# Fewer units with 16-row inverses in a chunked linear recurrence, and new step lists around it

## The chip, the core and the metric

The kernel runs on one core of one Trainium2 chip. The metric is the device time of one execution in microseconds (us). PE is TensorE (matmuls; PEld its weight loads), DVE VectorE, ACT ScalarE, POOL GpSimd, SP the queue that issues the DMAs. The granted clock is TensorE's clock as a share of its full 2.4 GHz.

## The reference

Three stages follow each other. The first is the one that the change touches; per batch b (4), head h (8) and step t of 768, with a state of 40 x 40:

```
y[t]  = r[t] @ state
Sa    = state @ a[t]
state = state * w[t] - outer(Sa, b[t]) + outer(v[t], k[t])
```

The second mixes positions and channels: u = x + (xT U V)T, then u + relu(u W1) W2, with U and V of rank 32 and 4 x 320 hidden channels. The third is an attention with four experts, of which each position takes two. U, V, W1 and W2 arrive as 64-bit floats and are converted on the chip.

## The kernel before

**Units and chunks.** The sequence is cut into 12 chunks of C = 64 steps. A chunk has two units, one per pair of batches: unit u belongs to chunk c = u // 2, and there are NU = 24. A unit holds 16 heads (8 columns p of 2 partition halves r). Four units make a group g (GU = 4), so chunks 0 and 1 are group 0, chunks 2 and 3 group 1, and so on to group 5.

**front(u)**, line 153 on, needs no state. Its 9 pieces are: the decay product Q by a scan (line 164), the inverse decay G (172), ga (177), bkt (180), all on DVE; then transposes of G (188) and of bkt (198) on PE; then the two 32 x 32 diagonal blocks and the block below them, pd (215), copied by ACT into LX, m21 and, for groups below HALVES, los (217 to 220); then pk (227), which POOL masks (230). Loads for unit u + 2 are issued along the way.

**lanes(g)**, line 233, inverts the triangular blocks of a whole group on DVE. After a transpose (237) each step s multiplies and adds (249, 251), one block per partition lane, and it ends with memsets and a transpose into tf (262). With g < HALVES a 32 x 32 block is treated as two 16 x 16 blocks, m = 2, and there are 14 steps; otherwise 30. Every yield ends a step.

**core(u)**, line 265, is the part that carries the state. pw (275) takes the old state X and v. Then, for the first and the second 32 rows (i = 0, 1): with g < HALVES a product with the 16-row inverse (pa, 297), a copy into U (300), a product with the block los between the halves (304), a copy into w (307), and in either form the product with tf (311) and a copy into U (314). For i = 1 the product with m21 (287) stands first. At the end px (321, 326) adds up the new state and DVE scales it into sv (328), which the next chunk's pw reads. That makes 10 steps with HALVES covering g, and 6 without.

**outs(u)**, line 332, has 6 steps and makes the output: transposes pv (339), pz (347), pn (360) masked by DVE into uvt (363), py (372, 376) scaled into x (380).

**The order** is written out by hand. PE, DVE, ACT and POOL run their instructions in program order; only the DMA issues on SP are placed by the framework. For each chunk a string gives the steps: A and B are the cores of the two units, p and q the outs of the two batch pairs (behind by one chunk and more), f the next piece of the fronts of later units, u the next weight conversion, x the products with U. Behind each letter that the second string names, one step of the oldest unfinished lanes is taken. A group's lanes become available with the last front piece of its fourth unit (line 405); what of it is left when its first chunk begins is run in one go (line 447). FIRST holds chunks 0 to 3, STEADY 4 to 6, TAIL 7 to 11. The front of the first four units and lanes(0) run before the first chunk.

**Weight conversions**, Mix.weights (line 545): 15 of them before the recurrence ends. Step u number i issues the load of the next one, finishes the one before (511, then its put: an ACT copy and a POOL subtraction), and converts its own: four DVE instructions (500, 501, 504, 505), an ACT one (502) and a POOL addition (506), which the next step's 511 waits for. The last one is finished after the recurrence.

Of the kernel before, what the change touches and what calls it, by code (L numbers as in the profile page):

```python
# [15 lines left out]
AF = mybir.ActivationFunctionType  # L16
# [12 lines left out]
PP = 8  # L29
WLEN = PP * (C + 1)  # L30
LDW = 3 * PP * C + WLEN
HP = PP // 2
GU = 4
# [5 lines left out]

HALVES = 2
FIRST = (('ABffABffABfffABffABffABfffABffABfffABABffff', ''),
         ('ABppffABfABppffABfABqqfABffABqqfABfppABABfffff', 'Ap'),
         ('ABqqfABppfABffABppfABfABqqfABffABqqppfABABfffff', 'AB'),
         ('ABqqfABppABfABppfABfABqqABfABqqppfABABffff', 'AB'))
STEADY = ('ABqqppfABfppfABfqqABfqqppfABABffff', 'ABf')
TAIL = (('ABqqppfABfppfABfqqABfqqppfABABffffu', 'ABf'),
        ('ABuqqppABuppABuqqABqqppABAB', 'ABp'), ('ABuqqppABuppABuqqABqqppABAB', 'ABp'),
        ('ABuqqppuxABuppxxABuqquxABqqppxABABxx', 'ABp'), ('ABuqqppuxABuppxABuqqxABqqppABAB', 'ABp'))  # L50


def recurrence(ctx, tc, ld, vin, rv, ident, xs, keep, wpool, mix):

    nc = tc.nc
# [53 lines left out]
    def zeros():  # L109

        for t in [x[:, 0] for x in sv[:2]] + [x[:, :, :, D:] for x in uv] + sbd + rpt:
# [3 lines left out]
    xf = [x.rearrange("p c f -> p (c f)") for x in xs]  # L115
    o = NC // 4 * DM
    los = [x[:, a:a + PP * 32].rearrange("p (q t) -> p q t", t=32)
           for a in [o + LDW + PP * 32 * k for k in range(3)] + [o + LDW - PP * 32] for x in xf]

    def edges(ts):  # L120
        for t in ts:
            nc.gpsimd.memset(t[:, :, :16], 0.0)

    edges(los[:6])

    BK, GA, PC, LX, M21, TF = {}, {}, {}, {}, {}, {}

# [15 lines left out]
    def copy_v(u):  # L143
        for r in range(2):
            z = slice(64 - 64 * r, 128 - 64 * r)
            nc.scalar.activation(uv[u % 4][z, :, r, :D], sv[u % 4][64 * r:64 * r + 64, 1], AF.Copy)
# [6 lines left out]
    def front(u):  # L153
# [64 lines left out]
        nc.scalar.activation(m21, pd[:, :, 1], AF.Copy)  # L218
        if g < HALVES:
            nc.scalar.activation(los[u][:, :, 16:], pd[:, :, 0, 16:], AF.Copy)  # L220
# [12 lines left out]
    def lanes(g):  # L233
# [3 lines left out]
        nc.vector.transpose(Lf, LX[g].rearrange("p t x -> p (t x)"))  # L237
        m = 2 if g < HALVES else 1
        h = 32 // m
# [25 lines left out]
    def core(u):  # L265

        g, uu = divmod(u, GU)
        c, bp = divmod(u, NBP)
        ga, bk, tf, X, U = GA[u], BK[u], TF[g], sv[u % 4], uv[u % 4]
        pw = ps.tile([128, PP, D], F32, tag=f"c{bp}", bufs=1, name=f"pw{u}")  # L270
        for p in range(PP):
            for k in range(2):
                for r in range(2):
                    q = slice(64 * r, 64 * r + 64)
                    nc.tensor.matmul(pw[q, p], ga[q, k, p], X[q, k, p], start=p == k == 0, stop=k == 1,  # L275
                                     skip_group_check=True)
        w0 = const.tile([128, PP, D], F32, tag="w0", bufs=2, name=f"w0{u}")
        nc.scalar.activation(w0, pw, AF.Copy)
        yield

        for i in range(2):
            qs = [slice(64 * r + 32 * i, 64 * r + 32 * i + 32) for r in range(2)]
            if i:
                for p in range(PP):
                    for r in range(2):
                        q0 = slice(64 * r, 64 * r + 32)
                        nc.tensor.matmul(pw[qs[r], p], M21[u][q0, p], U[q0, p, r, :D], start=False, stop=True,
                                         skip_group_check=True)
                nc.scalar.activation(w0, pw, AF.Copy)
                copy_v(u)  # L290
                yield
            if g < HALVES:

                pa = ps.tile([128, PP, D], F32, tag="f", bufs=6, name=f"pa{u}_{i}")
                for p in range(PP):
                    for q in qs:
                        nc.tensor.matmul(pa[q, p], tf[q.start:q.start + 16, uu * PP + p], w0[q.start:q.start + 16, p],
                                         start=p == 0, stop=True, skip_group_check=True)
                for r in range(2):
                    nc.scalar.activation(U[qs[r], :, r, :D], pa[qs[r]], AF.Copy)  # L300
                yield
                for p in range(PP):
                    for r, q in enumerate(qs):
                        nc.tensor.matmul(pw[q, p], los[u][q.start:q.start + 16, p], U[q.start:q.start + 16, p, r, :D],
                                         start=False, stop=True, skip_group_check=True)
                for q in qs:
                    nc.scalar.activation(w0[q], pw[q], AF.Copy)
                yield
            for p in range(PP):
                for r in range(2):  # L310
                    nc.tensor.matmul(pw[qs[r], p], tf[qs[r], uu * PP + p], w0[qs[r], p], start=p == 0,  # L311
                                     stop=True, skip_group_check=True)
            for r in range(2):
                nc.scalar.activation(U[qs[r], :, r, :D], pw[qs[r]], AF.Copy)
            yield
        if c < NC - 1:

            px = ps.tile([128, PP, D], F32, tag=f"c{bp}", bufs=1, name=f"px{u}")
            for r in range(2):
                q = slice(64 * r, 64 * r + 64)  # L320
                nc.tensor.matmul(px[q], ident[q, q], X[q, 0], start=True, stop=False, skip_group_check=True)
        yield
        if c < NC - 1:
            for p in range(PP):
                for r in range(2):
                    nc.tensor.matmul(px[64 * r:64 * r + D, p], bk[:, p, r], U[:, p, r, :D], start=False, stop=True,
                                     skip_group_check=True)
            nc.vector.tensor_tensor(sv[(u + NBP) % 4][:, 0], px,  # L328
                                    PC[u + NBP][:, :, None].to_broadcast([128, PP, D]), op=OP.mult)
        yield  # L330
# [52 lines left out]
    def run(*seqs):  # L383
        for seq in seqs:
            for _ in seq:
                pass
# [10 lines left out]
    def body(v):  # L397

        if v >= NU:
            return  # L400
        pieces = head(v + 1) if v != GU - 1 else iter(())
        for k in range(5):
            next(pieces, None)
            next(FR[v])
            if k == 4 and v % GU == GU - 1:
                LN.append(lanes(v // GU))
            yield

    def cores(bp):
        for u in range(bp, NU, NBP):  # L410
            yield from core(u)
# [23 lines left out]
    run(head(0))  # L435
    for v in range(GU):
        run(body(v))
    edges(los[6:])
    run(LN.pop())
    seqs = {"A": cores(0), "B": cores(1), "p": outputs(0), "q": outputs(1),  # L440
            "f": chain(head(GU), *[body(v) for v in range(GU, NU)]),
# [3 lines left out]
    for c in range(NC):  # L445
        while 2 * c // GU not in TF:
            run(LN.pop(0))
        steps, along = FIRST[c] if c < len(FIRST) else STEADY if 2 * c + AHEAD + NBP < NU else TAIL[c - NC]
        for x in steps:
# [474 lines left out]
def tile_kernel(ctx, tc, ld, vin, rin, U, V, w1, w2, qk, vg, wo, out):  # L924
# [6 lines left out]
    with ExitStack() as kctx:  # L931
# [3 lines left out]
        with ExitStack() as rctx:  # L935
            recurrence(rctx, tc, ld, vin, rin, ident, xs, keep, wpool, mix)
# [59 lines left out]
```

## Time and profile before

| what | value |
|---|---|
| three runs | 926.45, 921.86, 915.11 us; median 921.86 |
| the profiled execution | 912.26 us; its span 910.5 us |
| PE busy | 862.1 us, 95% of the span |
| DVE busy | 584.5 us, 64% |
| ACT busy | 478.7 us, 53% |
| POOL busy | 217.2 us, 24% |
| mean granted clock | 0.972 |
| recurrence (to its last product) | 0 to 430.8 us |

Spans are counted from the first instruction. A row of the windows view gives a stretch, its length, the busy time of each engine with the number of instructions, the granted clock, the mean busy share of the DMA engines and their GB/s. A row of a timeline gives start, duration, engine, line, operation, output <- inputs, shapes and the count of merged instructions; in square brackets how long the engine was idle before and what ended that.

### The profile page before, as it was taken

Reading aid. Unit: us, or ns where it says so; the run is one execution under the profiler, and the core shown is the slowest. Engines: PE = TensorE matmul, PEld = TensorE weight load, DVE = VectorE, ACT = ScalarE, POOL = GpSimd, SP = SyncE. Lnnn points to the kernel's source line nnn. Section 1 sums busy time; section 2 is a strip of 40 time slices with the busy share of each in tenths; the row PEclk is TensorE's granted clock in tenths of the full one; section 3 lists DMA queues with packets and bytes.
Section 4 is the critical chain, followed back from the end, with each engine's and each line's share of the span. In section 5 each row is a group of like instructions: output and inputs, shape, how many; then the busy total and the mean of one; then the engine's idle time right before and its main releaser. Section 6 shows DMA issues by size and latency. Waiting matters only on the chain.

```text
span 910.5 us, 31479 instructions
## 1 busy us (share of the span) xinstructions
PE 862.1 (95%) x13668; PEld 736.6 (81%) x13668; DVE 584.5 (64%) x1352; ACT 478.7 (53%) x1109; POOL 217.2 (24%) x245
## 2 busy tenths in 40 slices
PE   5599999999999989999999999999999999999997
PEld 4589888899899978888777888878778889797875
DVE  8867657789879688664662423232237886878874
ACT  5386656845665535554332423222237767766772
POOL 6111111001010103441341322020122633344330
PEclk9889879999999987999999999999999999999999
DMA  5232212212221123221100010000000000010001
GB/s 164 64 109 87 62 54 62 77 54 62 84 76 38 48 66 88 81 78 55 52 29 1 22 35 1 0 1 1 1 0 2 1 30 15 2 44 1 30 15 44
DMA packets 25386, 39.51 MB, mean 43 GB/s; under 512 B 5792, under 2 KB 12576, under 8 KB 25248
## 3 DMA queue, kind: packets, MB, share of 16 engines
q1 hardware_dynamic: 25248, 37.51, 13.7%
q8 instruction: 107, 1.75, 0.8%
q14 instruction: 31, 0.25, 0.1%
HBM read 33.56 MB, written 3.93 MB: 41 GB/s over the span
## 4 chain that ended last, share of the span: by engine, by line
PE 74%; DVE 9%; ACT 7%; issue 4%; POOL 2%; DMA 1%; SPq 0%; ACTq 0%; POOLq 0%; DVEq 0%
PE pn L360 5%; PE po L891 4%; PE pw L275 4%; PE tp L878 3%; PE ph L691 3%; PE pa L710 3%; PE pa L709 3%; PE ph L688 3%; PE pa L708 3%; PE ph L689 3%; PE ph L687 3%; PE pw L311 2%; PE pb L198 2%; PE py L372 2%; PE pd L215 2%
## 5 line engine op out<-in xcount | busy, mean ns | idle before, releaser
L695 DVE SCALAR_TENSOR_TENSOR hl<-ph,hh 128x512 fp32r<-128x512 f32 x60 | 41.1, 690 | 117.1 <-ACT hh L694 116.3
L861 POOL TENSOR_TENSOR P<-P,sm 128x128 f32<-128x128 f32 (+2 forms) x92 | 82.7, 929 | 126.5 <-DVE sm L851 114.3
L230 POOL TENSOR_TENSOR ga<-ga,mask 128x512 f32<-128x512 f32 x24 | 34.1, 1422 | 263.5 <-ACT ga L229 263.5
L694 ACT ACTIVATE hh<-ph 128x512 fp32r<-128x512 f32 x60 | 35.3, 597 | 112.1 <-PE pa L710 107.0
L842 ACT ACTIVATE P<-ps,mx 128x640 f32<-128x640 f32 (+4 forms) x96 | 60.5, 634 | 22.6 <-DVE mx L840 14.6
L840 DVE CUSTOM_DVE_ANT_0 ps<-ps,neg 128x640 f32<-128x640 f32 (+4 forms) x96 | 59.1, 639 | 7.6 <-PE ps L838 6.4
L249 DVE TENSOR_TENSOR tmp<-lt 128x84 f32<-128x84 f32 (+14 forms) x148 | 55.2, 373 | 3.1
L360 PE MATMUL pn<-rpt,uvt 128*128 128x128 f32 x384 | 52.6, 294 | 4.2 <-ACT uvt L340 3.2
L878 PE MATMUL tp<-ident,P 128*128 128x128 f32 x336 | 52.0, 275 | 2.3 <-DVE sm L849 0.9
L275 PE MATMUL pw<-sv,ga 64*64 64x40 f32 x1536 | 50.3, 232 | 4.0 <-DVE sv L328 3.8
L275 PEld LDWEIGHTS pw<-sv,ga 64*64 64x64 f32 x1536 | 49.1, 142 | 5.0 <-DVE sv L328 4.4
L251 DVE TENSOR_TENSOR lt<-lt,tmp 128x84 f32<-128x84 f32 (+14 forms) x148 | 49.6, 335 | 5.1
L360 PEld LDWEIGHTS pn<-rpt,uvt 128*128 128x128 f32 x384 | 47.9, 203 | 5.7 <-ACT uvt L340 4.8
L363 DVE TENSOR_TENSOR uvt<-pn,mask 128x512 f32<-128x512 f32 x48 | 32.2, 685 | 29.6 <-PE pn L360 27.7
L878 PEld LDWEIGHTS tp<-ident,P 128*128 128x128 f32 x336 | 39.5, 140 | 9.6 <-issue 2.2
L710 PE MATMUL pa<-hh,w 128*128 128x512 f32 x120 | 47.0, 392 | 0.0
L688 PE MATMUL ph<-ul,w 128*128 128x512 f32 x120 | 46.8, 390 | 0.2 <-DVE ul L677 0.2
L709 PE MATMUL pa<-hl,w 128*128 128x512 f32 x120 | 47.0, 391 | 0.0
L687 PE MATMUL ph<-uh,w 128*128 128x512 f32 x120 | 45.8, 391 | 1.2 <-ACT uh L676 1.2
L689 PE MATMUL ph<-uh,w 128*128 128x512 f32 x120 | 46.7, 389 | 0.0
L891 PE MATMUL po<-pt,vals 128*64 128x256 f32 (+3 forms) x320 | 45.1, 397 | 0.4 <-DVE pt L884 0.4
L724 POOL TENSOR_TENSOR t<-t,ul 128x512 f32<-128x512 f32 x12 | 15.4, 1302 | 120.2 <-DVE t L723 120.1
(218 smaller groups left out, 2311.6 us busy)
## 6 DMA issues: line engine op xcount, KB each, us to landing
ld<-in_ld SPq DMA_DIRECT2D x132, 80.0 KB
sv<-in_vin SPq DMA_DIRECT2D x48, 80.0 KB
rpt<-in_rin SPq DMA_DIRECT2D x48, 80.0 KB
out<-o SPq DMA_DIRECT2D x24, 160.0 KB
ld<-in_ld SPq DMA_DIRECT2D x44, 81.2 KB
ld<-in_w SPq DMA_DIRECT2D x4, 512.0 KB
ld<-in_w SPq DMA_DIRECT2D x5, 320.0 KB
room<-in_w SPq DMA_DIRECT2D x5, 320.0 KB
```

The lines of the kernel that those rows point to most:

```text
L275: nc.tensor.matmul(pw[q, p], ga[q, k, p], X[q, k, p], start=p == k == 0, stop=k == 1, skip_group_check=True)
L360: nc.tensor.matmul(pn[:, p], ut[:, h * HP + p], rp[:, :, h * HP + p], start=p == 0, stop=True, skip_group_check=True)
L687: nc.tensor.matmul(ph, w[:, 0, f], uh[:, ft], start=ft == 0, stop=False)
L688: nc.tensor.matmul(ph, w[:, 0, f], ul[:, ft], start=False, stop=False)
L689: nc.tensor.matmul(ph, w[:, 1, f], uh[:, ft], start=False, stop=False)
L709: nc.tensor.matmul(pa[ft], w[:, o:o + m], hl, start=False, stop=False)
L710: nc.tensor.matmul(pa[ft], w[:, 2 * DM - FT[2][0] + o:2 * DM - FT[2][0] + o + m], hh, start=False, stop=last)
L840: nc.vector.tensor_tensor_reduce(ps[:, :k], ps[:, :k], neg[:, S - k:], -1.0, 3e38, op0=OP.add, op1=OP.min, accum_out=mx[:, i:i + 1])
L842: nc.scalar.activation(P[blk][:, off[i] - off[i0]:off[i + 1] - off[i0]], ps[:, :k], AF.Exp, bias=mx[:, i:i + 1], scale=-1.0, accum_out=sm[ ...
L861: nc.gpsimd.tensor_tensor(p, p, sm[:, i:i + 1].to_broadcast([128, w]), op=OP.mult)
L878: nc.tensor.transpose(pt[:, j - j0], P[:, c:c + 128], ident)
L891: nc.tensor.matmul(po[64 * r:64 * r + 64, s0:w], VS[b][:, j, HD * e:HD * e + HD], PT[r][:, j, s0:], start=j == 0, stop=j == i1 - 1, skip_g ...
```

## The change

HALVES falls from 2 to 1, so group 1 (units 4 to 7) uses 32-row inverses like the groups behind it; only group 0 keeps the 16-row form. The los tiles shrink from eight to four, and the late memset of two of them goes. In the 16-row form the two copies of pw into w, one per 32 rows, become one over all rows. The strings of chunks 0 to 3 are new: the cores of chunks 2 and 3 have 6 steps, the letters f stand at other places (24, 13, 15, 13 of them in place of 23, 16, 15, 10), and the lanes go along with more letters. In the strings of chunks 7 to 11 the letters u number 0, 2, 2, 6, 6 in place of 1, 3, 3, 5, 4.

```diff
@@ -39,15 +39,15 @@
 
 
 
-HALVES = 2
-FIRST = (('ABffABffABfffABffABffABfffABffABfffABABffff', ''),
-         ('ABppffABfABppffABfABqqfABffABqqfABfppABABfffff', 'Ap'),
-         ('ABqqfABppfABffABppfABfABqqfABffABqqppfABABfffff', 'AB'),
-         ('ABqqfABppABfABppfABfABqqABfABqqppfABABffff', 'AB'))
+HALVES = 1
+FIRST = (('ABfffABfffABfffABfffABfffABfffABfffABfffABAB', 'AB'),
+         ('ABppffABfABppffABfABqqfABfABqqfABfppABABfff', 'ABpq'),
+         ('ABqqppffABfppffABfqqfABfqqppffABABfffff', 'ABf'),
+         ('ABqqppffABfppfABfqqfABfqqppfABABfffff', 'ABf'))
 STEADY = ('ABqqppfABfppfABfqqABfqqppfABABffff', 'ABf')
-TAIL = (('ABqqppfABfppfABfqqABfqqppfABABffffu', 'ABf'),
-        ('ABuqqppABuppABuqqABqqppABAB', 'ABp'), ('ABuqqppABuppABuqqABqqppABAB', 'ABp'),
-        ('ABuqqppuxABuppxxABuqquxABqqppxABABxx', 'ABp'), ('ABuqqppuxABuppxABuqqxABqqppABAB', 'ABp'))
+TAIL = (('ABqqppfABfppfABfqqABfqqppfABABffff', 'ABf'),
+        ('ABuqqppABppABuqqABqqppABAB', 'ABp'), ('ABuqqppABppABuqqABqqppABAB', 'ABp'),
+        ('ABuqqppuxABuppxxABuqquxABuqqppxABABxx', 'ABp'), ('ABuqqppuxABuppuxABuqqxABuqqppABAB', 'ABp'))
 
 
 def recurrence(ctx, tc, ld, vin, rv, ident, xs, keep, wpool, mix):
@@ -115,13 +115,13 @@
     xf = [x.rearrange("p c f -> p (c f)") for x in xs]
     o = NC // 4 * DM
     los = [x[:, a:a + PP * 32].rearrange("p (q t) -> p q t", t=32)
-           for a in [o + LDW + PP * 32 * k for k in range(3)] + [o + LDW - PP * 32] for x in xf]
+           for a in [o + LDW + PP * 32 * k for k in range(HALVES * GU // 2)] for x in xf]
 
     def edges(ts):
         for t in ts:
             nc.gpsimd.memset(t[:, :, :16], 0.0)
 
-    edges(los[:6])
+    edges(los)
 
     BK, GA, PC, LX, M21, TF = {}, {}, {}, {}, {}, {}
 
@@ -303,8 +303,7 @@
                     for r, q in enumerate(qs):
                         nc.tensor.matmul(pw[q, p], los[u][q.start:q.start + 16, p], U[q.start:q.start + 16, p, r, :D],
                                          start=False, stop=True, skip_group_check=True)
-                for q in qs:
-                    nc.scalar.activation(w0[q], pw[q], AF.Copy)
+                nc.scalar.activation(w0, pw, AF.Copy)
                 yield
             for p in range(PP):
                 for r in range(2):
@@ -435,7 +434,6 @@
     run(head(0))
     for v in range(GU):
         run(body(v))
-    edges(los[6:])
     run(LN.pop())
     seqs = {"A": cores(0), "B": cores(1), "p": outputs(0), "q": outputs(1),
             "f": chain(head(GU), *[body(v) for v in range(GU, NU)]),
```

## Rows read from the trace of the kernel before

**Rows 1.** windows, chunks 0 to 4 and 8 to 11: us, then busy by engine.
```profile
41.90:72.44 30.54, 29.76 (x920) 26.44 (x920) 20.41 (x25) 25.12 (x63) 3.82 (x3) 0.86 0.35 101
72.44:111.87 39.43, 38.13 (x1091) 34.54 (x1086) 26.93 (x50) 26.47 (x63) 4.01 (x3) 0.91 0.25 72
111.87:155.78 43.91, 42.14 (x1186) 37.87 (x1184) 29.80 (x59) 27.11 (x63) 4.80 (x3) 0.88 0.20 59
155.78:192.35 36.57, 35.09 (x1110) 31.45 (x1108) 28.22 (x62) 24.65 (x58) 2.53 (x2) 1.00 0.21 63
192.35:221.37 29.02, 28.99 (x857) 26.38 (x854) 26.32 (x56) 17.07 (x41) 2.60 (x2) 1.00 0.24 71
...
307.65:333.70 26.05, 21.72 (x633) 19.80 (x629) 23.38 (x61) 12.51 (x28) 4.28 (x6) 1.00 0.27 79
333.70:365.69 31.99, 31.01 (x633) 28.73 (x633) 25.89 (x56) 13.98 (x30) 7.30 (x6) 0.68 0.25 66
365.69:392.40 26.71, 26.05 (x663) 21.35 (x661) 18.75 (x35) 15.48 (x34) 11.30 (x13) 1.00 0.31 92
392.40:430.82 38.42, 36.23 (x886) 31.98 (x884) 18.80 (x33) 18.50 (x40) 10.13 (x12) 1.00 0.19 61
```

**Rows 2.** windows, the stretches after a TensorE stall.
```profile
118.40:129.00 10.60, 10.54 (x228) 9.56 (x230) 4.63 (x6) 6.11 (x15) 0.00 (x0) 0.52 0.22 65
333.70:354.00 20.30, 20.30 (x336) 19.42 (x338) 14.72 (x33) 6.61 (x14) 4.51 (x4) 0.51 0.24 63
```

**Rows 3.** timelines of VectorE and then TensorE, end of chunk 8.
```profile
316.39 0.35 DVE L511 SCALAR_TENSOR_TENSOR ld<-Q,ld 128x192 f32<-128x192 f32 x1
...
323.12 0.35 DVE L511 SCALAR_TENSOR_TENSOR ld<-invhot,ld 128x192 f32<-128x192 f32 x1
...
333.16 0.48 DVE L328 TENSOR_TENSOR sv<-px,pc 128x320 f32<-128x320 f32 x1
...
328.49 1.43 PE L326 MATMUL px<-uv,bk 128*40 128x40 f32 x64
333.70 6.91 PE L275 MATMUL pw<-sv,ga 64*64 64x40 f32 x128 [3.79 <-DVE sv L328]
```

**Rows 4.** timelines of VectorE and then TensorE, end of chunk 10.
```profile
385.25 0.49 DVE L511 SCALAR_TENSOR_TENSOR ld<-invhot,ld 128x320 f32<-128x320 f32 x1 [1.71 <-POOL ld L506]
...
390.80 1.10 DVE L328 TENSOR_TENSOR sv<-px,pc 128x320 f32<-128x320 f32 x2 [0.81 <-PE px L326]
...
392.40 3.93 PE L275 MATMUL pw<-sv,ga 64*64 64x40 f32 x128
```

**Rows 5.** timeline of TensorE in chunk 3 (start us, us, what, idle before).
```profile
152.32 0.66 PE L188 MATMUL pt<-ident,G 128*128 128x128 f32 x4
...
155.78 3.88 PE L275 MATMUL pw<-sv,ga 64*64 64x40 f32 x128
...
162.17 1.34 PE L297 MATMUL pa<-w,tf 16*32 16x40 f32 x64
...
176.94 1.66 PE L304 MATMUL pw<-uv,x 16*32 16x40 f32 x62 [0.20 <-ACT uv L300]
```

**Rows 6.** timeline of all engines, end of chunk 1 and start of chunk 2.
```profile
109.20 1.23 DVE L164 TENSOR_TENSOR_SCAN Q<-ld,onehot 128x520 f32<-128x520 f32 x1
...
112.82 2.22 POOL L230 TENSOR_TENSOR ga<-ga,mask 128x512 f32<-128x512 f32 x1 [5.63 <-ACT ga L229]
113.83 1.25 DVE L249 TENSOR_TENSOR tmp<-lt 128x28 f32<-128x28 f32 x1
...
115.12 0.19 DVE L251 TENSOR_TENSOR lt<-lt,tmp 128x28 f32<-128x28 f32 x1
...
118.46 0.76 PE L297 MATMUL pa<-w,tf 16*32 16x40 f32 x27 [1.06 <-DVE tf L262]
```

**Rows 7.** windows of chunk 4, line 249 and then line 251 alone.
```profile
192.35:221.37 29.02, 6.04 (x18) 1.00 0.24 71
...
192.35:221.37 29.02, 5.92 (x18) 1.00 0.24 71
```

## The prediction

> **What bounds the kernel now.** I read the page first (busy shares and granted clock over the span), then TensorE's waits, then a table of windows cut at the first pw matmul (line 275) of every chunk, then timelines around the waits. The windows' columns are the stretch, its length, the busy time of PE, PEld, DVE, ACT and POOL with counts, the granted clock and the DMA share and rate. The reader is to see three regions in [rows 1]. In a steady chunk (4) TensorE is busy for 28.99 of 29.02 us and VectorE for 26.32, so TensorE bounds it with VectorE close behind. Chunks 0 to 3 take 30.54 + 39.43 + 43.91 + 36.57 = 150.45 us; here units 0 to 7 use the 16-row form and the clock is below full in three of them. Chunks 8 to 11 hold no front, yet take 26.05 + 31.99 + 26.71 + 38.42 = 123.17 us, and chunk 9 at clock 0.68 does the same TensorE work as chunk 8.
>
> A low clock is dear. After two stalls the granted clock stands near 0.5, the 1.2 GHz level, for most of 10.6 and 20.3 us [rows 2]. The pw group takes 6.91 us there [rows 3] and 3.93 us at full clock [rows 4], 1.76 times, so each microsecond at the low level loses 0.43. From the mean clocks the time at the low level was 2(1 - 0.91) x 39.43 = 7.1 us in chunk 1, 10.5 in chunk 2 and 20.5 in chunk 9, and the losses are 3.1, 4.5 and 8.8 us.
>
> **Part 1: units 4 to 7 lose the 16-row steps.** Each chunk 2 and 3 drops two pa groups (1.34 us for 64 matmuls) and two los groups (1.34 to 1.9 us; one is in the rows) [rows 5]: about 5.8 us of TensorE per chunk, 11.6 in all, on the engine that bounds. Their copies go too: 16 ScalarE copies per chunk of some 0.43 us, which TensorE sometimes waited for (0.20 us at the los group [rows 5]). Chunk 2 also loses its first stall, 1.06 us for the transposed inverses tf [rows 6], because the new lists finish group 1's inverse inside chunk 1; with that stall goes the low clock behind it, 4.5 us.
>
> The price is VectorE. A 32-row inverse has 30 steps of two instructions where the 16-row one has 14. In chunk 4, 18 such steps took 6.04 + 5.92 us [rows 7], 0.66 a step, 0.72 with the gap between instructions. All of group 1's steps but four now fall in chunk 1: 26 x 0.72 = 18.7, with the closing transpose and memsets 21.3 us, in place of 9.0 now (13 small steps and the opening transpose). One front costs VectorE 4.63 us, from 109.20 to 113.83 [rows 6], and TensorE 3.46, from 152.32 to 155.78 [rows 5]; a step "f" is a fifth: 0.92 and 0.70.
>
> **Part 2: the lists of chunks 0 to 3.** Steps "f" per chunk go from 23, 16, 15, 10 to 24, 13, 15, 13.
> Chunk 0: one more f (+0.7), and no f is left behind the last A and B, so the new state sv, which now queues on VectorE behind group 1's opening transpose and two steps, is bare: +1.2. Bounds: 0 if VectorE is early, +3.8 if sv is as late as in chunk 8 [rows 3]. I take +1.9.
> Chunk 1: VectorE needs 26.93 - 9.0 - 3 x 0.92 + 21.3 = 36.4 us. TensorE at full clock needs 38.13 - 3.1 - 2.1 = 33. VectorE takes over. At the share that it reaches in chunk 4 (0.91) that is 40; with its waits for ScalarE and TensorE I take 42, +2.6. Bounds 36.4 and 49.
> Chunk 2: 43.91 - 1.06 - 4.5 - 5.8 = 32.5 for TensorE; VectorE has some 28, but bunched in the second half with group 2's steps: +1.5. I take 34, -9.9.
> Chunk 3: 36.57 - 5.8 - 1.1 (ScalarE waits) + 2.1 = 31.8 for TensorE; VectorE 28.22 + 2.8 = 31, at 0.91 34. I take 34, -2.6.
> The sum is -8.0. The single w copy in group 0 in place of two saves 0.43 us of ScalarE four times a chunk in chunks 0 and 1, beside other work; two memsets fewer on GpSimd at the start are 0.2 us each, off the path. Both at nothing: TensorE or VectorE covers them, and without the cover they would give back 3.4 and 0.4 us. The loads that the fronts issue on SP move with them by at most three f; they stay two units ahead.
>
> The row at the end of chunk 1 shows a step of 28 elements taking 1.25 us while GpSimd's masking ran, and its partner 0.19 without [rows 6]. The Trainium skill (SBUF — State Buffer, Who interferes with whom) says that a VectorE instruction with two SBUF inputs and a GpSimd instruction reading SBUF exclude each other; the trace agrees. By that rule each of chunk 1's three maskings could now hold one step for another 1.06 us, and the chunk would be 45 and not 42.
>
> **Part 3: conversions of the last chunks.** The 16 steps u go from 1, 3, 3, 5, 4 (chunks 7 to 11) to 0, 2, 2, 6, 6.
> Chunk 8: the last sv starts on VectorE some 3 us after px ended, and TensorE stands for 3.79 us [rows 3]. Of VectorE's work ahead of it two conversions go, 316.39 to 318.66 and 323.12 to 325.98, 5.1 us, and the first one (1.3) comes in. VectorE then still waits for TensorE's pn at 318.4, so sv moves by 2.7 us, not 3.8, and 1.1 us of stall stays: -2.7.
> Chunk 9: if the clock holds, -8.8.
> Chunk 10: six conversions instead of five, and larger ones, 15.7 us against 12.1. VectorE was already waiting 1.71 us for GpSimd inside one, and had only 0.81 us to spare before sv [rows 4]. The extra one stands ahead of the uvt masking and sv: 2.2 us of its own, 1.2 of wait for GpSimd, 1.2 from the larger ones, less 0.8, is 3.8; part is gained where VectorE now idles. I take +3, bounds 0 and +5.
> Chunk 11: two more conversions, 5.5 us, ahead of the last py products, where VectorE idles up to 4 us at a time: +3, bounds 0 and +5.5.
> A stall of 3 us before chunk 11 may drop the clock: 0 to 8.8, at even odds for the lesser loss seen (4.5): +2.5. The sum is -3.0.
>
> **Total.** -8.0 - 3.0 = -11 us. The profiled execution took 912.26 us (span 910.5 and 1.8 around it) and would take 901; the median of the three runs shown is 921.86, 9.6 us more. Against the median: 911 us.
>
> **Rivals.**
> A, both regions come out clean: chunks 0 to 3 reach their floors, 31.3 + 36.4 + 32.5 + 31.8 = 132, -18.5; the tail gives -3.8 - 8.8 + 3 = -9.5. That is -28 and 894 us. For it: chunk 4 runs with no stall at 0.91 of VectorE. Against: chunk 1 would want VectorE without a gap. Chance 0.22.
> B, the stall is only moved: chunk 10 now ends as chunk 8 did and chunk 11 runs at the low clock for the whole 20.5 us: +6.3 on the forecast, 917 us. For it: the 0.81 us of slack. Against: stalls of about 1 us in chunks 9 and 11 left the clock full. Chance 0.17.
> C, slower: in chunk 1 TensorE waits for VectorE so often that the clock goes to the low level and stays. Its 33 us then become 33 x 1.76 = 58, +16 on my 42, and the total is +5: 927 us. It decides from 26 us at the low level on (11/0.43). For it: shorter stalls brought 7 to 10 us in chunks 1 and 2. Against: a slow TensorE is a busy one, and after 10 us the clock came back. Chance 0.10.
> The forecast, 911, keeps 0.51, with its own range 903 to 918.
>
> **How the numbers follow.** The measurement tells about 2% from no change, 18.4 us here, so faster means under 903.4. A gives most of its chance, the forecast a little: 0.25. Slower by 2% means over 940.3, beyond C: 0.04, for a C with a poor tail. Within 2%: 0.71. The range 896 to 926 leaves out half of A and half of C.
>
> **What would show it.** Right: no line 297 in chunks 2 and 3; 30 steps of line 249 in chunk 1 or just before it, VectorE over 0.85 busy there; no stall for tf at chunk 2's start; full clock in chunk 9; a longer TensorE wait for sv at the end of chunk 10. Wrong: chunk 1 under 38 us (towards A) or over 48 at a low clock (C), chunk 9 still at a low clock, or chunk 11 over 45 us (B).

## The result, and the profile after

The changed kernel took 913.26 us (median, 901.82 to 917.2) and the kernel before 920.97 (915.11 to 926.45), 14 runs each on one chip: 7.7 us less between the medians. The ratio is 0.9892, interval 0.9858 to 0.9925: 9.9 us less (6.9 to 13.1), faster by 1% and within the 2% that count as no change. The ratio leaves out the five longest runs of the changed kernel (915.44 to 917.2 us) as slow ones and none of the kernel before, which widens the difference. The forecast was 911, with a range of 896 to 926.

The profiled execution took 914.89 us, its span 913.2 us. Its page gives the busy times from TensorE to GpSimd:

```profile
PE 858.9 (94%) x13156; PEld 731.5 (80%) x13156; DVE 600.6 (66%) x1383; ACT 460.6 (50%) x1065; POOL 215.8 (24%) x241
```

TensorE is busy for 3.2 us less than before and VectorE for 16 us more. From line 307 on the code's line numbers are one lower than before, from 438 on two lower (sv is L327, pn L359, the finishing step of a conversion L509).

The windows view, cut at the first pw of each chunk, answers to [rows 1]: chunks 0 to 4, then 8 to 11.

```profile
44.11:79.45 35.34, 32.80 (x953) 28.48 (x953) 26.85 (x32) 23.81 (x59) 5.09 (x4) 0.80 0.37 106
79.45:118.39 38.94, 36.54 (x956) 32.97 (x957) 34.60 (x81) 22.25 (x52) 2.76 (x2) 0.87 0.18 54
118.39:153.27 34.88, 31.82 (x924) 28.65 (x924) 27.41 (x48) 20.01 (x47) 3.89 (x3) 1.00 0.22 66
153.27:192.24 38.97, 37.92 (x949) 34.55 (x948) 31.37 (x68) 19.75 (x47) 2.81 (x3) 0.82 0.23 66
192.24:221.54 29.30, 29.30 (x850) 26.38 (x849) 28.13 (x59) 16.54 (x40) 2.47 (x2) 1.00 0.25 71
...
308.73:331.73 23.00, 21.89 (x639) 19.99 (x635) 19.49 (x49) 11.69 (x26) 2.31 (x3) 1.00 0.18 50
331.73:353.91 22.18, 21.82 (x632) 19.94 (x632) 18.58 (x53) 11.55 (x26) 1.95 (x3) 1.00 0.27 75
353.91:385.48 31.57, 26.60 (x663) 21.33 (x661) 23.18 (x39) 16.78 (x36) 14.08 (x13) 1.00 0.31 84
385.48:434.25 48.77, 44.76 (x884) 39.60 (x885) 25.01 (x44) 20.50 (x44) 14.65 (x18) 0.79 0.24 72
```

Chunk 2 is 9.0 us shorter and at full clock; chunk 9 is 9.8 shorter at 1.00 in place of 0.68. Chunk 10 is 4.9 longer, and chunk 11 10.3 longer at 0.79. Chunk 3 has fewer matmuls than in [rows 1], but takes longer at 0.82. A steady chunk (4) takes 29.30 us.

TensorE's waits, from its timeline (the bracket gives the idle time before and what ended it):

```profile
79.45 3.93 PE L275 MATMUL pw<-sv,ga 64*64 64x40 f32 x128 [0.82 <-DVE sv L327]
...
118.39 3.93 PE L275 MATMUL pw<-sv,ga 64*64 64x40 f32 x128 [0.68 <-DVE sv L327]
...
152.28 1.06 PE L198 MATMUL pb<-ident,bkt 128*128 128x128 f32 x8 [3.06 <-DVE bkt L180]
...
331.73 3.93 PE L275 MATMUL pw<-sv,ga 64*64 64x40 f32 x128 [0.93 <-DVE sv L327]
...
385.48 6.66 PE L275 MATMUL pw<-sv,ga 64*64 64x40 f32 x128 [2.25 <-DVE sv L327]
```

The stall for tf at the start of chunk 2 [rows 6] is gone; 0.68 us for sv is left. The 3.79 us before chunk 9 [rows 3] are 0.93. New are 3.06 us for bkt at the end of chunk 2, and 2.25 us for sv before chunk 11, behind which pw takes 6.66 us where it took 3.93 [rows 4].

The execution behind the rows of before (912.26 us) was shorter than each of the 14 timed ones. A second profile of the unchanged kernel (e1_before) has a span of 919.9 us. Its windows for chunks 0 and 3:

```profile
43.37:78.33 34.96, 33.91 (x920) 30.26 (x920) 20.38 (x25) 25.36 (x63) 3.81 (x3) 0.71 0.30 88
...
161.56:201.80 40.24, 39.20 (x1111) 35.72 (x1108) 28.24 (x62) 24.64 (x58) 2.53 (x2) 0.87 0.20 57
```

Against [rows 1] chunk 0 has a clock of 0.71 for 0.86 and is 4.4 us longer, chunk 3 0.87 for 1.00 and 3.7 longer. So both are compared. The last column is wider: it is the mean of the profiled executions with the new lists less the mean of those with the old. Up to chunk 7 these are this one, e2_head, e5_after, e6_five and e11_dvecopy against before, e1_before, e3_tail and e4_copy; from chunk 8 on this one, e3_tail, e5_after, e7_onef, e8_laneslater and e9_head2 against before, e1_before, e2_head and e4_copy. The next section says what these runs are.

| stretch | predicted | after less rows 1 | after less e1_before | mean, new lists less old |
|---|---|---|---|---|
| before chunk 0 | 0 | +2.2 | +0.7 | +0.4 |
| chunk 0 | +1.9 | +4.8 | +0.4 | +3.6 |
| chunk 1 | +2.6 | -0.5 | -0.2 | -1.1 |
| chunk 2 | -9.9 | -9.0 | -9.2 | -9.2 |
| chunk 3 | -2.6 | +2.4 | -1.3 | -0.3 |
| chunks 4 to 7 | 0 | +1.2 | +1.3 | +1.5 |
| chunk 8 | -2.7 | -3.1 | -3.2 | -3.3 |
| chunk 9 | -8.8 | -9.8 | -9.8 | -10.0 |
| chunk 10 | +3 | +4.9 | +4.8 | +4.8 |
| chunk 11, with the clock drop | +5.5 | +10.3 | +10.3 | +9.6 |
| behind the recurrence | 0 | -0.7 | -0.5 | -0.5 |
| sum | -11.0 | +2.7 | -6.7 | -4.4 |

The two columns of single executions differ by chunks 0 and 3 above all, where the same code ran at other clocks. The end of chunk 7 came at 307.65 us in before, 310.62 in e3_tail, 314.52 in e4_copy and 316.97 in e1_before, and with the new lists at 304.17 to 310.55. So e1_before is the longest of four, and the mean is the column to read. It gives 4.4 us less where the timed runs give 7.7 to 9.9; where the rest comes from these profiles do not show.

### The profile page after: what moved, and what is told of

The parts are those of the page before. It is cut to its first block, busy times and chain, and to the rows that moved or that the text cites. A ratio compares the mean times of both kernels' runs of the same rounds, so it can differ in the third digit from the quotient of the medians.

```text
span 913.2 us, 30426 instructions
## 1 busy us (share of the span) xinstructions
PE 858.9 (94%) x13156; PEld 731.5 (80%) x13156; DVE 600.6 (66%) x1383; ACT 460.6 (50%) x1065; POOL 215.8 (24%) x241
## 3 DMA queue, kind: packets, MB, share of 16 engines
HBM read 33.56 MB, written 3.93 MB: 41 GB/s over the span
## 4 chain that ended last, share of the span: by engine, by line
PE 65%; DVE 7%; ACT 4%; POOL 2%; issue 1%; DMA 0%; ACTq 0%; POOLq 0%; DVEq 0%
PE po L889 4%; PE pw L275 4%; PE pn L359 3%; PE tp L876 3%; PE ph L689 3%; PE pa L708 3%; PE ph L686 3%; PE pa L707 3%; PE pa L706 3%; PE ph L687 3%; PE ph L685 3%; PE py L371 2%; PE ps L836 2%; PE ps L835 2%; PE py L375 2%; PE pa L703 2%
## 5 line engine op out<-in xcount | busy, mean ns | idle before, releaser
L249 DVE TENSOR_TENSOR tmp<-lt 128x58 f32<-128x58 f32 (+9 forms) x164 | 61.7, 376 | 3.5
L251 DVE TENSOR_TENSOR lt<-lt,tmp 128x58 f32<-128x58 f32 (+9 forms) x164 | 56.5, 345 | 5.6
L359 PE MATMUL pn<-rpt,uvt 128*128 128x128 f32 x384 | 54.0, 299 | 4.9 <-ACT uvt L339 3.8
L275 PE MATMUL pw<-sv,ga 64*64 64x40 f32 x1536 | 52.5, 237 | 4.7 <-DVE sv L327 4.7
L275 PEld LDWEIGHTS pw<-sv,ga 64*64 64x64 f32 x1536 | 51.1, 147 | 6.7 <-DVE sv L327 5.7
L359 PEld LDWEIGHTS pn<-rpt,uvt 128*128 128x128 f32 x384 | 49.2, 208 | 6.5 <-ACT uvt L339 5.6
```

What stands on the lines that cost most here:

```text
L249: latest["dve"] = nc.vector.tensor_tensor(tv, block(s + 1, s, n, 1).to_broadcast([128, m, n, s]), block(s, 0, 1, s).to_broadcast([128, m, ...
L359: nc.tensor.matmul(pn[:, p], ut[:, h * HP + p], rp[:, :, h * HP + p], start=p == 0, stop=True, skip_group_check=True)
```

## The experiments

Each ratio is to runs of the kernel before on the same chip. e1 to e4 shared one chip, e5 to e8 a second, e9 to e11 a third; e12 had runs of its own.

**The two halves of the change.** e1_before is the kernel before, unchanged. e2_head has all of the change but the TAIL lists, e3_tail only those, and e4_copy only the single copy into w:

```diff
-                for q in qs:
-                    nc.scalar.activation(w0[q], pw[q], AF.Copy)
+                nc.scalar.activation(w0, pw, AF.Copy)
```

> The kernel before, unchanged, profiled once more. Its one profiled execution took 912.3 us, under every one of the 14 timed runs (915 to 926). Theory A (the profiled execution was a lucky one, with fewer stretches at the low clock): this profile takes 917 to 925 us and its mean clock is below 0.972, and the extra time stands in stretches at the 1.2 GHz level inside the recurrence. Theory B (the profile is taken in another way and is always shorter than the timed runs): 910 to 914 us and clock 0.972 again. Ratio 1.00 either way.

> All of the change but the lists of chunks 7 to 11, which stay as before. My theory as predicted (first region -8, last region -3): -8 us against before, ratio 0.991. Rival, that the first region gives nothing (chunks 0 and 3 longer by what chunk 2 saves, as the profile after shows) and the tail all of it: 0 us, ratio 1.00. Rival, that the tail's lists cost and the first region carries more than the whole gain: -10 to -13 us, ratio 0.986 to 0.989.

> The kernel before with only the new lists of chunks 7 to 11. My theory as predicted: -3 us, ratio 0.997, the stall at the end of chunk 8 nearly gone and a new one of some 3 us at the end of chunk 10. Rival, that the stall is only moved and the low clock with it: +2 us, ratio 1.002. Rival, that the tail carries the whole gain: -8 to -10 us, ratio 0.99.

> The kernel before with only the two copies of pw into w made one, for units 0 to 7 (32 of 1,065 or so ScalarE copies become 16, 0.43 us each). As predicted (hidden beside TensorE): 0 us, ratio 1.00. Rival, that ScalarE is on the path in chunks 1 to 3, where TensorE waited for its copies some 3 us in all: -2 to -5 us, ratio 0.995 to 0.998.

Measured: e1_before 1.0017 (0.9985 to 1.0048); e2_head 0.9954 (0.9928 to 0.9979), that is -4.2 us of 918.59 (-6.6 to -1.9); e3_tail 1.0007 (0.9976 to 1.0038), +0.6 us (-2.2 to +3.5); e4_copy 0.9996 (0.9966 to 1.0027). The windows of e3_tail for chunks 10 and 11:

```profile
355.73:387.31 31.58, 27.70 (x662) 22.77 (x660) 23.18 (x39) 16.79 (x36) 14.09 (x13) 0.95 0.31 83
387.31:438.65 51.34, 45.09 (x884) 40.34 (x885) 25.09 (x44) 20.41 (x44) 14.67 (x18) 0.80 0.22 69
```

Chunks 8 and 9 show their gain in full there (22.92 and 22.19 us, where e1_before has 26.22 and 32.01), and chunks 10 and 11 give it back: 31.58 and 51.34, where e1_before has 26.75 and 38.51. So the head (the lists and the inverses of chunks 0 to 3) gains, the tail (the lists of chunks 7 to 11) does not, and the copy does nothing that these runs can tell. e2_head meets none of its three expectations: its interval lies between the theory's 0.991 and the first rival's 1.00. The interval of e3_tail leaves out the theory's 0.997 and holds the 1.002 of the rival that the stall is only moved.

**The whole again, and five conversions in chunk 10.** e5_after is the changed kernel. e6_five moves one u from chunk 10 to chunk 9 (0, 2, 3, 5, 6):

```diff
-        ('ABuqqppABppABuqqABqqppABAB', 'ABp'), ('ABuqqppABppABuqqABqqppABAB', 'ABp'),
-        ('ABuqqppuxABuppxxABuqquxABuqqppxABABxx', 'ABp'),
+        ('ABuqqppABppABuqqABqqppABAB', 'ABp'), ('ABuqqppABuppABuqqABqqppABAB', 'ABp'),
+        ('ABuqqppuxABuppxxABuqquxABqqppxABABxx', 'ABp'),
```

> The changed kernel, unchanged, beside the others of this call. It measured 0.9892 of before; with the new first region alone 0.9954 was measured on another chip. If the new lists of chunks 7 to 11 add nothing on top of the new first region: 0.995. If they add what the first measurement says: 0.989. Its profile has a wait for sv of 2 to 3 us ahead of chunk 11 and a low clock behind it.

> The changed kernel with the conversions of chunks 8 to 11 as 2, 3, 5, 6 in place of 2, 2, 6, 6: the sixth of chunk 10 goes to chunk 9. Theory (the stall at the end of chunk 10 is the extra conversion ahead of sv on VectorE, and the low clock of chunk 11 follows from that stall): no wait for sv there over 1 us, clock of chunk 11 near 1.00, chunk 10 at 27 to 28 us and chunk 11 at 39 to 41, chunk 9 up to 1 us longer, in all 10 to 13 us less than the changed kernel. Rival (conversions two places later are late whatever the list, the flush after chunk 11 waits for them): 0 to 4 us less.

Measured: e5_after 0.9907 (0.9871 to 0.9943), e6_five 0.9914 (0.9884 to 0.9944): no gain, where the theory of e6_five expected 10 to 13 us. Chunks 9 and 11 of e6_five:

```profile
333.46:360.59 27.13, 24.49 (x633) 22.50 (x633) 21.99 (x58) 12.52 (x28) 4.03 (x5) 0.87 0.27 80
...
390.51:435.62 45.11, 40.27 (x886) 35.74 (x884) 24.74 (x42) 20.26 (x44) 14.90 (x18) 0.89 0.24 70
```

The 2.25 us before chunk 11 are gone from its timeline. But a wait of 2.63 us for ScalarE's uvt has come up in chunk 9, at clock 0.87, and inside chunk 11 TensorE waits 2.67 us for ScalarE's w; the clock was 1.00 up to that wait and 0.56 in the 11.5 us behind it. With sixteen steps u in chunks 8 to 11, taking one out of one place only made another late.

**The end of chunk 2.** From the timeline of the changed kernel, rows of DVE and POOL ahead of the 3.06 us wait:

```profile
148.59 0.37 DVE L251 TENSOR_TENSOR lt<-lt,tmp 128x198 f32<-128x198 f32 x1
...
149.41 1.35 POOL L230 TENSOR_TENSOR ga<-ga,mask 128x512 f32<-128x512 f32 x1 [10.17 <-DVE sv L327]
149.68 1.32 DVE L251 TENSOR_TENSOR lt<-lt,tmp 128x210 f32<-128x210 f32 x1
...
150.92 1.21 DVE L180 TENSOR_TENSOR bkt<-ld,Q 128x1024 f32<-128x1024 f32 x1
```

bkt, for which TensorE stands, is queued behind the inverse steps of group 2 and the two sv. One of these steps (L251 with 210 elements) took 1.32 us beside GpSimd's masking (1.35 us), the one before it with 198 only 0.37: 0.95 us of the 3.06. Then the granted clock (windows):

```profile
152.28:162.00 9.72, 9.72 (x178) 9.47 (x180) 8.15 (x18) 1.75 (x4) 0.00 (x0) 0.58 0.24 72
```

Two edits, each by itself and then together. e7_onef takes the last f of chunk 3 away, so that the steady chunks meet each front at the piece where they did before. e8_laneslater lets group 2's steps in chunk 2 go along with fewer letters. e9_head2 has both.

```diff
 e7: FIRST[3]
-         ('ABqqppffABfppfABfqqfABfqqppfABABfffff', 'ABf'))
+         ('ABqqppffABfppfABfqqfABfqqppfABABffff', 'ABf'))
 e8: FIRST[2]
-         ('ABqqppffABfppffABfqqfABfqqppffABABfffff', 'ABf'),
+         ('ABqqppffABfppffABfqqfABfqqppffABABfffff', 'AB'),
```

> The changed kernel with one f less at the end of chunk 3, so that every later chunk meets the fronts at the same pieces as before. In the profile after, chunks 4 to 6 take 29.29 us where they took 28.73, both with TensorE busy throughout. Theory (a front's two pb groups, split by other matmuls, cost TensorE time at each change of shape): chunks 4 to 6 at 28.73 again, 1.7 us less in all. Rival (the los tiles' place or another wait): 29.29 stays and the time is the same within 0.3 us but for the shorter chunk 3.

> The changed kernel with group 2's inverse taken along with A and B alone in chunk 2, not with f: about nine steps of 0.72 us, 6.5 us of VectorE, move from the end of chunk 2 into chunk 3. Theory (the wait of 3.06 us for bkt at the end of chunk 2 and the low clock in chunk 3 are VectorE's lag under those steps): that wait goes, chunk 3 keeps its clock at its start; but VectorE then has some 38 us in chunk 3, so chunks 2 and 3 together change by -4 to +2 us. Rival (the wait comes from the loads or ScalarE): it stays at about 3 us and the two chunks take 74 us as now.

> The two edits of the first region together on the changed kernel: group 2's inverse along with A and B alone in chunk 2, and one f less at the end of chunk 3. With the first alone TensorE still waited 1.83 us for G at the start of chunk 4 and that chunk ran at clock 0.81, 35.4 us. Theory (VectorE's lag sits in the last f of chunk 3, and every such wait brings a low clock): that f is gone from there, no wait over 1 us, chunk 4 at 28.7 to 30 us, chunks 2 to 6 together 153 to 156 us where the changed kernel takes 161; 4 to 8 us less than the changed kernel, ratio 0.981 to 0.987. Rival (the lag moves on once more): a wait and a low clock in chunk 4 or 5, ratio 0.987 as with either edit alone.

Measured: e7_onef 0.9875 (0.9827 to 0.9923) and e8_laneslater 0.9873 (0.9826 to 0.9921), beside 0.9907 of e5_after, with intervals that overlap its own, so the times alone do not show a gain of either; e9_head2 0.985 (0.9807 to 0.9894). Chunks 2, 3 and 4 of e8_laneslater, and TensorE's wait before chunk 4:

```profile
116.13:148.33 32.20, 31.81 (x924) 28.64 (x924) 23.98 (x38) 20.03 (x47) 3.72 (x3) 1.00 0.25 71
148.33:182.76 34.43, 31.85 (x950) 28.75 (x949) 32.01 (x62) 20.00 (x47) 4.27 (x4) 1.00 0.26 75
182.76:218.13 35.37, 35.37 (x849) 32.23 (x848) 30.27 (x68) 16.62 (x39) 1.59 (x2) 0.81 0.19 59
```

```profile
182.17 0.66 PE L188 MATMUL pt<-ident,G 128*128 128x128 f32 x4 [1.83 <-DVE G L172]
```

The wait for bkt fell to 0.39 us and chunk 3 ran at full clock, 4.3 us shorter than in e5_after (38.72); chunks 2 and 3 together are 7.0 us shorter, more than the 4 expected. But the steps not taken stood in chunk 3, and now 1.83 us for G came before chunk 4: clock 0.81, 6.1 us lost against e5_after's 29.30. Chunks 3 and 4 of e7_onef, and of both kernels the transposes of bkt at the end of chunk 4 (first e7_onef):

```profile
155.22:193.07 37.85, 37.23 (x945) 34.14 (x946) 30.36 (x66) 18.91 (x45) 2.81 (x2) 0.82 0.23 68
193.07:221.80 28.73, 28.73 (x855) 26.23 (x852) 26.16 (x56) 17.07 (x40) 2.65 (x2) 1.00 0.25 73
```

```profile
218.76 1.10 PE L198 MATMUL pb<-ident,bkt 128*128 128x128 f32 x8
```

```profile
215.09 0.66 PE L198 MATMUL pb<-ident,bkt 128*128 128x128 f32 x4
...
218.26 0.66 PE L198 MATMUL pb<-ident,bkt 128*128 128x128 f32 x4
```

With one f less the transposes of bkt stand together (1.10 us for eight) and not as two groups with px between them (0.66 each), and the steady chunk is back at 28.73. The Trainium skill (TensorEngine Tiling (Array Packing), Key Properties) says that changing the tile mode drains TensorE; the trace agrees so far that a stretch with one more split of groups took 0.57 us more, 0.22 of them in these rows, but it does not show the drain apart.

Both edits together (e9_head2, chunks 2 to 4, then 11):

```profile
116.88:149.08 32.20, 31.81 (x924) 28.65 (x924) 23.97 (x38) 20.00 (x47) 3.72 (x3) 1.00 0.24 71
149.08:181.44 32.36, 31.31 (x945) 28.40 (x946) 29.94 (x60) 18.76 (x45) 2.63 (x3) 1.00 0.28 80
181.44:212.84 31.40, 29.41 (x854) 26.42 (x851) 29.97 (x67) 17.58 (x41) 3.00 (x2) 1.00 0.23 66
...
376.64:428.54 51.90, 48.43 (x884) 42.87 (x885) 25.17 (x44) 20.48 (x44) 14.67 (x18) 0.74 0.23 68
```

Chunks 2 to 4 take 95.96 us where e5_after takes 102.91, with no clock drop. The ratio lies where the theory of e9_head2 expected it (0.981 to 0.987), but its interval overlaps that of e5_after. The profiled execution was the longest of its six (909.01 us), and chunk 11 fell to 0.74 in it.

**The conversions.** VectorE's timeline at the end of chunk 10 of the changed kernel, which answers to [rows 4]:

```profile
376.43 0.69 DVE L509 SCALAR_TENSOR_TENSOR ld<-Q,ld 128x512 f32<-128x512 f32 x1 [1.38 <-POOL ld L504]
...
377.92 1.39 DVE L502 TENSOR_SCALAR ld<-ld 128x320 int32<-128x320 int32 x1
...
383.35 1.27 DVE L362 TENSOR_TENSOR uvt<-pn,mask 128x512 f32<-128x512 f32 x2
384.55 0.47 DVE L379 TENSOR_TENSOR x<-py,x 128x320 f32<-128x320 f32 x1
384.95 0.87 DVE L327 TENSOR_TENSOR sv<-px,pc 128x320 f32<-128x320 f32 x2
...
387.02 0.33 DVE L502 TENSOR_SCALAR ld<-ld 128x320 int32<-128x320 int32 x1
```

In [rows 4] VectorE stood idle for 0.81 us before the last sv; here it comes to it from uvt and x without a gap. Inside the conversions it stands 1.38 us for GpSimd (L504), and line 502 takes 1.39 us while GpSimd's subtraction runs (L515, 1.27 us from 377.86) and 0.33 at the same size when GpSimd has nothing to do. In chunk 11 ScalarE carries the lateness on:

```profile
406.09 0.47 ACT L601 ACTIVATE w<-ld 128x320 fp32r<-128x320 f32 x1 [2.40 <-DVE ld L509]
...
407.15 0.44 ACT L289 ACTIVATE w<-pw 128x320 f32<-128x320 f32 x1
```

The rounding copy L601 stands 2.40 us for VectorE's finishing step L509; w, which TensorE wants, is two instructions behind it on the same queue, after an ACT step (L500) of the next conversion. TensorE waited 0.74 us for that w.

e10_fewer is e9_head2 with two conversions left to behind the recurrence and the u at 2, 1, 2, 5, 4. e11_dvecopy is the changed kernel with the rounding copies of the conversions (lines 514 and 601) on VectorE in place of ScalarE, to take them out of w's way. e12_earlier is e9_head2 with all 15 conversions in the recurrence, the u at 3, 2, 2, 5, 4:

```diff
 e10 (its lists of chunks 7 to 11 left out)
-BEFORE = 15
+BEFORE = 13
 e11
+def put_split(nc, hi, lo, x):
+    nc.vector.tensor_copy(hi, x)
+    nc.gpsimd.tensor_tensor(lo, x, hi.bitcast(F32), op=OP.subtract)
...
-        split(self.tc.nc, w[:, 0, :n], w[:, 1, :n], A)
+        put_split(self.tc.nc, w[:, 0, :n], w[:, 1, :n], A)
...
-        nc.scalar.activation(w[:, :DM], A, AF.Copy)
+        nc.vector.tensor_copy(w[:, :DM], A)
 e12
-TAIL = (('ABqqppfABfppfABfqqABfqqppfABABffff', 'ABf'),
+TAIL = (('ABqqppufABfppfABfqqABfqqppfABABufffuf', 'ABf'),
...
-        ('ABuqqppuxABuppxxABuqquxABuqqppxABABxx', 'ABp'), ('ABuqqppuxABuppuxABuqqxABuqqppABAB', 'ABp'))
+        ('ABuqqppuxABuppxxABuqquxABqqppxABABxx', 'ABp'), ('ABuqqppuxABuppxABuqqxABqqppABAB', 'ABp'))
```

> As the run before, and the conversions spread anew: two steps u in chunk 7, then 1, 2, 5, 4, and the last two of the fifteen left to the channel mix, where VectorE is busy 70 of 189 us. Theory (the tail's gain is real and is lost only to conversions crowded into chunks 10 and 11): chunk 8 at 23 to 24, chunk 9 at 22 to 24, chunk 10 at 27 to 28, chunk 11 at 38 to 40 at full clock, 110 to 116 us in all where the changed kernel takes 121 to 125; a further 6 to 12 us less, ratio 0.970 to 0.978. Rival (any conversion beside chunks 8 and 9 costs the wait for sv again): chunk 9 or 10 at a low clock, no gain over the run before.

> The changed kernel with the rounding copy of each converted weight on VectorE instead of ScalarE (23 copies of 0.4 to 0.6 us). In chunks 10 and 11 ScalarE stands up to 2.4 us at such a copy until VectorE has finished the weight, with the recurrence's copies behind it. Theory (ScalarE's queue is what carries the conversions to TensorE): the waits for uvt and w of 1 to 2.6 us in chunks 10 and 11 go, the wait for sv stays or grows by 1 us, clock higher, 3 to 8 us less. Rival (VectorE itself is the bound of the last two chunks): 12 more copies on it cost 0.4 us each, the wait for sv grows, 0 to 5 us more.

> The shorter lists of chunks 2 and 3 as in e9_head2, all 15 conversions inside the recurrence, but the 16 steps u numbered 3, 2, 2, 5, 4 in chunks 7 to 11 (the changed kernel has 0, 2, 2, 6, 6). Theory 1, what counts is how many conversions stand in chunks 10 and 11: the last sv of chunk 10 waits for TensorE again and not the other way round, chunk 10 takes 27 to 29 us and chunk 11 37 to 40 at full clock, as in e10_fewer; chunk 7 and 8 grow by at most 1.5 us together, since VectorE has some 6 us free in chunk 7; ratio to the kernel before 0.970 to 0.979. Theory 2, leaving two conversions behind the recurrence is what helped e10_fewer (more VectorE time free everywhere in the tail): the stall appears at the end of chunk 9 or 10 all the same, chunk 11 over 45 us, ratio 0.983 to 0.988 as for e9_head2. Theory 3: the early conversions stand before a front's pieces and make chunk 8 wait: chunk 7 and 8 grow by 3 us and more, ratio 0.980 to 0.983.

Measured: e10_fewer 0.9775 (0.9728 to 0.9821), 898.15 us; e11_dvecopy 0.9958 (0.9929 to 0.9987), above the 0.9907 and 0.9892 of the changed kernel, with overlapping intervals; e12_earlier 0.9743 (0.9711 to 0.9775), 896.99 us, the lowest ratio, though its interval overlaps that of e10_fewer. TensorE's wait before chunk 11 in e11_dvecopy:

```profile
382.47 7.05 PE L275 MATMUL pw<-sv,ga 64*64 64x40 f32 x128 [6.99 <-DVE sv L327]
```

With the copies on VectorE the waits for ScalarE in chunk 10 (1.64 and 0.91 us in the changed kernel) went, but the wait for sv grew from 2.25 to 6.99 us, and the chunk from 31.57 to 33.03. So VectorE's queue is what is late ahead of sv; that ScalarE only passes the lateness on is argued from this and from the 2.40 us above. e10_fewer, chunk 11 and all that follows:

```profile
372.41:410.29 37.88, 36.08 (x886) 31.96 (x885) 18.50 (x32) 18.18 (x40) 9.65 (x13) 1.00 0.26 68
410.29:893.60 483.31, 466.80 (x2621) 380.82 (x2620) 263.63 (x716) 229.63 (x534) 145.06 (x157) 1.00 0.05 17
```

Chunk 11 is at full clock, 14.0 us shorter than in e9_head2; the two conversions left out come back behind the recurrence, 4.6 us (483.31 for 478.76). e12_earlier, chunks 8, 10 and 11 and all that follows:

```profile
302.36:330.22 27.86, 24.28 (x639) 22.27 (x635) 25.23 (x61) 12.97 (x29) 5.34 (x6) 0.88 0.32 91
...
353.79:380.53 26.74, 26.10 (x663) 21.40 (x661) 18.75 (x35) 15.48 (x34) 11.30 (x13) 1.00 0.32 92
380.53:418.83 38.30, 36.23 (x886) 31.99 (x884) 18.81 (x33) 18.48 (x40) 10.15 (x12) 1.00 0.21 61
418.83:897.70 478.87, 465.56 (x2621) 380.89 (x2620) 259.70 (x706) 229.14 (x530) 140.30 (x152) 1.00 0.05 16
```

Chunks 10 and 11 are what e1_before has (26.75 and 38.51), and nothing is paid at the end. It is paid in chunk 8, 4.9 us more than in e9_head2, by a new wait:

```profile
320.28 3.78 PE L359 MATMUL pn<-rpt,uvt 128*128 128x128 f32 x16 [2.64 <-ACT uvt L339]
```

So it is not how many conversions there are but how many stand in chunks 10 and 11. Theory 1 of e12_earlier holds there and in the ratio, but it gave chunks 7 and 8 at most 1.5 us more. Theory 3 is right that the early ones make chunk 8 late, and this is the next wait to work on (not tried).

## Why the prediction was right, and where it was not

**The sum.** 11 us were forecast and 9.9 (6.9 to 13.1) measured, 7.7 between the medians. The number came out, its parts only in part: chunks 2, 8 and 9 came as worked out, but by the means of the table the rest of the head took back nearly half of what chunk 2 gained, and chunks 10 and 11 took back all that chunks 8 and 9 gained. That leaves -4.4. So it is partly luck that 9.9 lies so near to 11.

**Head, -8.0.** By the means of the table it came to -5.1 down to chunk 7, and by the times of e2_head to -4.2 (-6.6 to -1.9). Against e1_before alone it would be -8.2, but that is the longest of the four executions. With e3_tail the timed halves sum to -3.6, short of the whole on two chips (-9.9, and -8.6 with e5_after: -11.9 to -5.3). e5_after ran on another chip than the halves, and the halves do not simply add: in e2_head the unchanged tail took 125.44 us, where e1_before has 123.49. Why the whole gains more than its halves stays open.

Chunk 2, -9.9: right in size and cause. No 16-row group is left, the stall for tf went and the clock held (-9.2, alike in every execution to half a microsecond). Chunk 0, +1.9: +3.6 in the mean, near its bound of 3.8. Its bare sv is there with 0.82 us, under the 1.2 supposed; but in all five executions with the new lists, and in none of the four with the old, TensorE also waits some 0.77 us for bkt, 4.5 us into the chunk. The prediction did not count that wait. Chunk 1, "VectorE takes over": not so. VectorE was busy for 34.60 us, 0.89 of the chunk (36.4 were forecast), but TensorE for 36.54, at a clock of 0.87, and its longest wait inside the chunk was 1.37 us for a copy of ScalarE (L300). The chunk took 38.94 for 42. The maskings did not make it 45 either: only two fell in the chunk (x2 of its row; three were counted). Each held one step, 1.36 us for a step of 240 elements where the one before took 0.40, and 0.88 us for one of 30 elements.

A masking held a step at the end of chunk 2 too, the 1.32 us ahead of bkt. The wait for bkt there was not foreseen: the step that failed is "VectorE has some 28, but bunched in the second half ... +1.5", which left out that the last front piece of the chunk stands behind that bunch. It cost chunk 3 its clock, 38.97 us where 34 was forecast. With that wait at 0.39 us chunk 3 took 34.43 (e8_laneslater), and with one f less as well 32.36 (e9_head2). That -2.6 became -0.3 in the mean has a second reason: the 36.57 us that the forecast started from were the one execution of four with full clock there, and the others took 39.97 to 40.36. The 1.5 us of chunks 4 to 7 were forecast at nothing: the f, one more over the first four chunks, moved where each front is met (e7_onef).

**Tail, -3.0.** Chunk 8 (-2.7, measured -3.3) and chunk 9 (-8.8, measured -10.0) came as worked out, with 0.93 us of the 1.1 us of stall left. Chunk 10 (+3, bounds 0 to 5) came near its bound: +4.8. The term that failed is the clock drop, "0 to 8.8, at even odds for the lesser loss seen (4.5): +2.5". By the prediction's own rate chunk 11 was 2(1 - 0.79) x 48.77 = 20.5 us at the low level, a loss of 8.8: the upper end. The two conversions in chunk 11 themselves are then 10.3 - 8.8 = 1.5, less than the 3 given; worked out in the same way from e7_onef (0.92, 45.22 us) they are 3.6. The windows of the changed kernel show the level right behind the 2.25 us:

```profile
385.48:395.00 9.52, 9.52 (x184) 9.44 (x184) 2.29 (x6) 1.61 (x4) 1.83 (x3) 0.53 0.17 55
```

This is rival B, the stall only moved, in its place and by its mechanism; its sign, chunk 11 over 45 us, came with the signs for the forecast. It had 0.17. It put 6.3 us on the forecast; chunks 8 to 11 came to +2.1 in place of -3.0, 5.1 more (+1.1 in the mean). The wait itself was foreseen ("a stall of 3 us", measured 2.25), so the even odds for the clock were the mistake. In all eight profiled executions with six steps u in chunk 11 its clock fell, to 0.74 to 0.92, and it took 44.8 to 51.9 us.

But the wait for sv is not the only place where it fell. In five of them (the changed kernel, e3_tail, e7_onef, e8_laneslater, e9_head2) that wait was 2.00 to 2.25 us, and in e7_onef the pw behind it still took 3.93 us; there the clock was 1.00 up to a second wait, inside chunk 11, and 0.87 from it on:

```profile
384.66 3.93 PE L275 MATMUL pw<-sv,ga 64*64 64x40 f32 x128 [2.06 <-DVE sv L327]
...
402.58 0.76 PE L310 MATMUL pw<-w,tf 32*32 32x40 f32 x32 [2.63 <-ACT w L289]
```

So it was in e5_after, with 0.84 us for sv and 2.61 for w, and in e6_five, with no wait for sv of 0.3 us or more and 2.67 for w. The conversions that stand in chunk 11 lose clock there too, where the prediction gave them their own time alone. With four steps u in chunk 11 and no wait for sv ahead of it (e10_fewer, e12_earlier) it took 37.9 and 38.3 us at 1.00. Rival A, a clean tail, came in e10_fewer, with chunks 8 to 11 at 1.00, but with another numbering of the u. Rival C, chunk 1 at the low level throughout, did not come: 0.87.

## What to carry to other kernels

Where stalls cost clock, work moved off one hand-over has to be followed to the next: count, chunk by chunk, what stands on each in-order engine ahead of the one instruction that the next chunk waits for. The same fifteen conversions gave 0.985 with steps u at 0, 2, 2, 6, 6 (e9_head2) and 0.9743 at 3, 2, 2, 5, 4 (e12_earlier), each against the kernel before on its own chip. VectorE has time in chunk 7 (21.9 of 28.7 us busy in e9_head2) and had only 0.81 us ahead of the last sv of chunk 10 [rows 4]. Compare several executions before a stage's length is taken for its cost: here a second one of the kernel before was the longest of four and would have made the head's forecast look exact.

## What was not expected of the hardware

The same instructions met other clocks in other executions: the kernel before had 0.86 and 0.71 in chunk 0, 1.00 and 0.87 in chunk 3, and spans of 910.5 and 919.9 us. Chunk 0 with the new lists took from 33.10 (e5_after) to 38.55 us (e6_five).

The length of a wait alone does not tell whether the clock falls. In e8_laneslater 1.83 us before chunk 4 left 0.81 over the chunk. In e10_fewer 2.10 us, 9 us into the same chunk, left it full (TensorE's timeline, then the windows view from that matmul on):

```profile
188.75 1.34 PE L310 MATMUL pw<-w,tf 32*32 32x40 f32 x64 [2.10 <-DVE tf L262]
```

```profile
188.75:200.00 11.25, 11.20 (x384) 10.37 (x384) 10.70 (x27) 8.45 (x21) 0.00 (x0) 1.00 0.13 36
```

A VectorE instruction with one input was also held by GpSimd: line 502 of a conversion, as shown for chunk 10. The Trainium skill (SBUF — State Buffer, Who interferes with whom) names tensor_scalar among the operations that can enter a two-port mode and then contend; the trace agrees: 1.39 us against 0.33 at the same size. The prediction had reckoned with this rule for the inverse's steps alone.
